# A kernel's head rearranged: the second load of V on SyncE, V's rows split over three engines, both W1 folds in front of the first MLP product

## The chip, the cores and the metric

The kernel runs on one core of one Trainium2 chip. A core has a matrix engine (TensorE, PE in the profile, with its weight loads as PEld), VectorE (DVE), ScalarE (ACT), GpSimd (POOL) and SyncE (SP). Each takes its instructions in order; semaphores connect them. DMAs are issued from the queues of SP, ACT and POOL. TensorE writes its products to PSUM, and DVE or ACT bring them from there to SBUF. The metric is the device time of the core in microseconds, as the median of several executions; smaller is better.

## The reference

The input x has 8 images of 3136 rows and 256 columns. What is computed is the real part of a two-dimensional Fourier transform, then a low-rank mixing over the rows, then an MLP over the columns with a residual:

```python
X = np.fft.fft(x, axis=1)
X = np.fft.fft(X, axis=2).real          # (8, 3136, 256)
xt = X.transpose(0, 2, 1)
h = xt @ U @ V                          # U (3136, 32), V (32, 3136)
u = X + h.transpose(0, 2, 1)
out = u + np.maximum(u @ w_ch1, 0.0) @ w_ch2   # 256 -> 1024 -> 256
```

## The kernel before

The 3136 rows are taken as 49 x 64 (`N1`, `N2`), and only 25 values of `k1` (`NK1`) are transformed, since the input is real; the other 24 follow by symmetry. The images go in four pairs. Every image passes these steps: a first transform over 49 rows, a turn of the layout into `g` (128 rows of 25 x 256), a transform over 64 rows that multiplies `g` with the table `T` and at the same time adds the low-rank part, and the MLP. Rows 0 to 63 of `T` are sine and cosine values; rows 64 to 127 are V, in two copies: as it is, in the columns 0 to 63 (the plus rows), and turned and with a sign on a part of the rows, in the columns 64 to 127 (the minus rows). Rows 64 to 127 of `g` hold `te`, the product of the image with U, repeated for all 25 `k1`: this repetition is called the spread. So the product of `g` and `T` gives u. It comes out in PSUM and is copied as bf16 to `q`.

The MLP works on chunks of 512 columns of `q`. `mlp1(chunk, t)` makes a quarter of the hidden layer, four products of 128x512 into a PSUM buffer `hps`, which ACT brings to `hT` with the ReLU (L385). `mlp2(chunk, t)` multiplies `hT` with `W2` and adds the residual from the tables `Bp` or `Bm` (L394, L397). The weights `W1p` (two halves of 512 columns, used by t = 0, 1 and by t = 2, 3) are not w_ch1 itself: the transform over the columns is folded into them by a product of the table `Q` with a half of w_ch1 (`w1_fold`, L668, four matmuls in fp32r) and a scaling by 0.5. `W2` is w_ch2 with its halves added and subtracted (`w2_fold`, L531).

The order is written out by hand (`tc.manual_schedule()`, L461): each engine takes its instructions as the Python code issues them. The code ahead of the loop (L463 to L722) is the head: it builds all tables, loads the weights and takes the first image as far as `q`. In the loop (L815) every step t of a chunk issues `mlp1`, the previous chunk's `mlp2` and then the functions that the list `at` holds for this step (L773 to L813): for the first pair, among others, the rest of the first image's transform (`s3b0`), the folds of W2 and the late tables.

What matters around the change, in the order of the code:

- V is loaded twice into `uv`, fp32 and 32 rows each, rows 64 to 95 (L495) and rows 96 to 127 (L627), both from POOL's queue. The second stands behind the one-element copy `gate` (L617), which waits for a table of DVE, and ahead of the load of W1's first half (L624).
- The table `T` gets its upper rows from PSUM by four DVE copies (L614), and its reversed half by one more (L660).
- The residual's angles are made on POOL, masked on DVE (`bp_mask`, L661) and taken through the sine on ACT (`bp_sin`, L688).
- A second one-element copy `gate` (L662) on POOL waits for a late row of `g0`.
- `w1_fold(0)` (L675) stands ahead of the products for `te` (`te_single`, L693).
- `v_rows` (L678) writes V's rows into `T`: `k1` 0 to 8 on ACT, 9 to 16 and 17 to 24 on POOL. Each call makes the plus rows by a cast, L681 or L684, and the minus rows by a multiply with the sign column `vs`, L682 or by `tg`, L514. The read goes through `Vk`, which steps by 49 fp32 elements.
- The first eight `k1` are multiplied in two passes, first with the 64 table rows, then with all 128 rows and `te` (L698 to L701), and moved to `q` in two parts, blk 0 by ACT and blk 1 by DVE (L702).
- `w1_late` (L706) runs behind the first `mlp1`: the second fold into two PSUM tiles of the transform's pool, its scaling by two DVE instructions, and the spread of `k1` 8 to 15 on DVE. POOL spreads `k1` 16 to 24 (L713) and then loads the next image (L716).
- `jio` and `Q` come from two SBUF pools. `kpool` and `pool` (for `tmp`) both end with the head, and the buffers of the loop (`q` of the other pair, `hT`, `ob`) lie over them; a buffer's first writer waits for the last readers of what lay there.
- PSUM buffers come from three pools of two: `bank2` (shared with `hps`), `bank_d` (the transform) and `bank_o` (shared with `mlp2`).

Of the kernel before, what the change touches and what calls it, by code (L numbers as in the profile page):

```python
# [11 lines left out]
FP32R = mybir.dt.float32r  # L12
I32 = mybir.dt.int32
# [9 lines left out]
def kernel(  # L23
# [51 lines left out]
    def copy_dve(o, i):  # L75
        nc.vector.tensor_copy(o, i)  # L76
# [352 lines left out]
    def tmp(shape, name, dt=FP32):  # L429
        return pool.tile(shape, dt, name=name, tag=name)  # L430
# [35 lines left out]
    next(loads)  # L466
    pio = tmp([P, 1], "pio", I32)
    nc.gpsimd.iota(pio[:], pattern=[[0, 1]], base=0, channel_multiplier=1)
    jio = kpool.tile([P, D], I32, name="jio", tag="jio")
    nc.gpsimd.iota(jio[:], pattern=[[1, D]], base=0, channel_multiplier=0)  # L470
    uv = kpool.tile([P, S], FP32, name="uv", tag="uv")
    uf = kpool.tile([P, 1024], FP32, name="uf", tag="uf")[:, 0:NK1 * R].rearrange("p (k r) -> p k r", r=R)
# [7 lines left out]
    def bank2(name):  # L480
        return psh.tile([P, 2, 512], FP32, tag="h", name=name)

    def bank_d(name):
        return psd.tile([P, 2, D], FP32, tag="ps", name=name)
# [108 lines left out]
        ts(an2[:, i], jf[0:PR, 0:32], pv[:, 6:7], pv[:, 7 + i:8 + i])  # L593
    mask_bits(an2[:], 16)
    mask_bits(jq[:], 16)
    Q = tmp([P, 3, P], "Q", FP32R)

    usv = us[:].rearrange("p k (r s) -> p k s r", s=2)
    upss = [bank2("uups") for i in range(2)]
# [12 lines left out]
    for i in range(4):  # L612
        k0, k1 = 8 * i, min(8 * i + 8, NK1)
        copy_dve(T[0:64, k0:k1, 0:64], tpss[i][0:64, 0:k1 - k0])  # L614

    gate = tmp([64, 4], "gate")
    nc.gpsimd.tensor_copy(gate[0:1, 0:1], an2[0:1, 0, 0:1])  # L617
# [6 lines left out]
        nc.gpsimd.dma_start(out=w, in_=moe_w_ch1.rearrange("(h p) j -> p h j", p=P)[:, :, c * 512:(c + 1) * 512])  # L624
        return w

    nc.gpsimd.dma_start(out=uv[96:128], in_=moe_V)  # L627
    w1_f = [load_w1(0)]

    g0 = gpool.tile([P, NK1, D], BF16, tag="g0", name="g")  # L630
# [27 lines left out]
    outs[1](copy_act)  # L658
    quarter_rows(g0, zts[1], 16, [copy_dve] * 6 + [copy_act] * 2)
    nc.vector.tensor_copy(T[0:64, :, 64:128], T[0:64, :, 63::-1])  # L660
    bp_mask()  # L661
    nc.gpsimd.tensor_copy(gate[32:33, 2:3], g0[32:33, 0, 80:81])  # L662

    teps = bank2("teps")
    for i in range(5):
# [9 lines left out]
    w1_fold(0, [w1ps[:, 0], w1ps[:, 1]])  # L675
    Vk = uv.rearrange("p (k2 k1) -> p k1 k2", k1=N1)

    def v_rows(lo, hi, act=False):  # L678
        l = max(lo, 1)
        if act:  # L680
            nc.scalar.copy(T[64:128, lo:hi, 0:64], Vk[64:128, lo:hi, :])  # L681
            nc.scalar.activation(T[64:128, l:hi, 64:128], Vk[64:128, N1 - l:N1 - hi:-1, :], AF.Copy, scale=vs[64:128])  # L682
        else:
            nc.gpsimd.tensor_copy(T[64:128, lo:hi, 0:64], Vk[64:128, lo:hi, :])  # L684
            tg(T[64:128, l:hi, 64:128], Vk[64:128, N1 - l:N1 - hi:-1, :], vs[64:128], None)

    v_rows(0, 9, True)
    bp_sin()  # L688
    nc.scalar.mul(W1p[0][:], w1ps[:], 0.5)
    v_rows(9, 17)  # L690
    v_rows(17, NK1)

    te_single(first, 0, lambda g, te: None, teps)  # L693
    s3b0 = list(s3_steps(first, 0, copy_alt))
    lines, move_part = s3b0.pop(0)
    groups = [(g, blk) for g in range(2) for blk in range(2)]
    pss = [bank("ps") for bank in [bank_d, bank_d, bank_o, bank_o]]
    for ps, (g, blk) in zip(pss, groups):  # L698
        lines(ps, g, blk, 64)
    for ps, (g, blk) in zip(pss, groups):  # L700
        lines(ps, g, blk, P, tes[0])  # L701
    for part in range(2):  # L702
        for ps, (g, blk) in zip(pss, groups):
            move_part(ps, g, blk, copy_dve if blk else copy_act, part)

    def w1_late():  # L706
        w1ps = [bank_d("w1ps").rearrange("p a d -> p (a d)") for blk in range(2)]
        w1_fold(1, w1ps)
        for blk in range(2):
            ts(W1p[1][:, blk], w1ps[blk], 0.5, None)  # L710
        spread([(nc.vector, 8, 16)])(g0, tes[0])

    spread([(nc.gpsimd, 16, NK1)])(g0, tes[0])  # L713
    idx0 = cpool.tile([PR, 8 * NP], I32, name="idx0")
    nc.gpsimd.iota(idx0[:], pattern=[[PR * 16, NP], [-1, 8]], base=48 * 16 + 15, channel_multiplier=-16)
# [57 lines left out]
    def plan(p):  # L773

        at = [[] for _ in range(NS)]

        def place(steps, lo, hi):
            steps = list(steps)
            for i, s in enumerate(steps):
                at[lo + i * (hi - lo) // len(steps)].append(s)  # L780

        def place_next(nx, a, gap, s3lo):

            s1 = list(s1_steps(nx, copy_act))
# [77 lines left out]
```

## Time and profile before

| what | value |
|---|---|
| median of 6 runs | 460.75 us (459.8 to 466.6) |
| profiled execution | 463.08 us, span 461.3 us |
| granted TensorE clock, mean | 0.991 |
| PE busy | 432.2 us, 94% of the span |
| ACT, DVE, POOL busy | 297.3, 225.0, 142.2 us |
| HBM read, written | 34.62 and 32.19 MB, 145 GB/s |
| share of the DMA engines, 13.5 to 15 us and 15 to 16.5 us | 0.4 and under 0.1 |
| PE busy between 30.8 and 36.9 us | 4.05 us of 6.10 |

The span runs from the first to the last instruction of the profiled execution; its own time has 1.8 us around it. Busy shares are means over stages with different limits: the head, up to about 37 us, has all engines at work in turn, while later PE is nearly always busy. The timeline gives for every line its start and its length in us, then engine, source line, operation, the tiles written and read with their shapes, the count, and in brackets the idle time of the engine ahead of it with what ended it. The waits give engine, line and releaser, then the total in us, how often, and the longest.

The operations of the head that the change moves, as the profile gives them:

| instruction | where | us |
|---|---|---|
| V cast, 64x576 | ACT | 1.22 |
| V times sign, 64x512 | ACT | 1.19 |
| V cast, 64x512 | POOL | 1.08 |
| V times sign, 64x512 | POOL | 2.06 |
| spread 64x1024 / 64x1152 | DVE / POOL | 1.03 / 1.49 |
| W1p scaling 128x512 from PSUM | DVE | 0.685 |
| W1p scaling 128x1024 from PSUM | ACT | 1.00 |
| second load of V, 392 KB | POOL queue | 0.60 to issue, 4.1 to land |
| one half of W1, 512 KB | POOL queue | 0.76 to issue, 4.6 to 4.9 to land |

### The profile page before, as it was taken

To read this page: it belongs to the slowest core of one execution; us is meant where nothing else is said; L and a number is where in the kernel's file an instruction comes from. 1 tells how busy PE (TensorE), PEld (TensorE's weight loads), DVE (VectorE), ACT (ScalarE), POOL (GpSimd) and SP (SyncE) were. 2 spreads that over 40 slices of the span, in tenths; PEclk is the share of its full clock that TensorE was granted. 3 is DMA by queue.
4 is the path that set the end of the run, shared out by engine and by line. 5 is a ranking of instruction groups with operands and counts; after the bars stand their busy time and mean duration, and the time that the engine had idled before them with its cause. 6 is when DMAs were issued, how large, how long until landed. Compare 5 with 4: busy or idle time off the path is not lost.

```text
span 461.3 us, 10592 instructions
## 1 busy us (share of the span) xinstructions
PE 432.2 (94%) x4217; PEld 309.7 (67%) x4217; DVE 225.0 (49%) x540; ACT 297.3 (64%) x426; POOL 142.2 (31%) x159
## 2 busy tenths in 40 slices
PE   3889996999989989999999989999999999999994
PEld 1756664777767767767767767776867777677663
DVE  7674567664336476455354386436254345111212
ACT  5776884777555666777465657777566655666662
POOL 7484535751330363452330354452220000000000
PEclk9799999999999999999999999999999999999999
DMA  8649754785492547673862447674752222222313
GB/s 149 149 135 164 212 153 110 207 207 171 134 251 56 155 121 233 182 209 116 196 173 70 111 155 215 167 234 128 182 128 66 68 62 65 70 73 72 91 47 92
DMA packets 59714, 64.35 MB, mean 139 GB/s; under 512 B 12902, under 2 KB 52624, under 8 KB 59504
## 3 DMA queue, kind: packets, MB, share of 16 engines
q1 hardware_dynamic: 49904, 42.28, 35.6%
q0 software_dynamic: 7280, 14.70, 13.8%
q10 hardware_dynamic: 2480, 6.69, 3.9%
q8 instruction: 33, 0.54, 0.5%
q14 instruction: 17, 0.14, 0.1%
HBM read 34.62 MB, written 32.19 MB: 145 GB/s over the span
## 4 chain that ended last, share of the span: by engine, by line
PE 65%; DMA 9%; DVE 7%; ACT 4%; SPq 4%; issue 2%; DVEq 0%; ACTq 0%
PE hps L383 27%; PE ops L394 27%; DMA out_dram<-ob 4%; PE ps L322 4%; SPq L409 4%; PE ops L397 3%; DMA xa<-in_x_dram 3%; ACT hT L385 2%; PE ps L184 2%; DVE g L76 2%; DMA g<-zturn 1%; DVE ob L405 1%; DVE q L76 1%; DVE yb L134 1%; DVE ob L404 1%
## 5 line engine op out<-in xcount | busy, mean ns | idle before, releaser
L385 ACT ACTIVATE hT<-hps 128x1024 bf16<-128x1024 f32 (+1 forms) x208 | 202.4, 976 | 122.5 <-PE hps L383 118.0
L394 PE MATMUL ops<-W,hT 128*128 128x256 bf16 x1568 | 224.7, 273 | 0.6 <-DVE W L532 0.3
L394 PEld LDWEIGHTS <-hT 128*128 128x128 bf16 x1568 | 145.1, 98 | 35.0 <-DVE ob L405 0.8
L404 DVE TENSOR_TENSOR ob<-ops,om 128x256 f32<-128x256 f32 (+1 forms) x102 | 42.2, 413 | 192.2 <-ACT om L403 183.8
L383 PE MATMUL hps<-q,W1p 128*128 128x512 bf16 (+1 forms) x448 | 105.0, 356 | 0.9 <-DVE q L76 0.6
L383 PE MATMUL hps<-q,W1m 128*128 128x512 bf16 x384 | 98.1, 379 | 0.5 <-ACT hT L385 0.5
L143 POOL TENSOR_TENSOR y<-xa,xb 98x1020 f32<-98x1020 f32 (+1 forms) x24 | 55.1, 2297 | 126.2 <-DMA xa<-in_x_dram 108.5
L76 DVE CAST q<-ps 128x512 bf16<-128x512 f32 (+3 forms) x121 | 64.4, 555 | 28.9 <-PE ps L322 27.6
L383 PEld LDWEIGHTS <-W1p 128*128 128x128 bf16 x448 | 40.3, 98 | 26.6 <-issue 1.7
L383 PEld LDWEIGHTS <-W1m 128*128 128x128 bf16 x384 | 35.3, 98 | 26.5 <-issue 1.4
L397 PEld LDWEIGHTS <-q 128*128 128x128 bf16 x392 | 38.4, 98 | 21.3 <-issue 0.6
L403 ACT COPY om<-ops 128x256 f32<-128x256 f32 (+1 forms) x102 | 37.1, 364 | 8.1 <-PE ops L394 7.7
L405 DVE TENSOR_TENSOR ob<-ops,om 128x256 f32<-128x256 f32 (+1 forms) x102 | 41.1, 403 | 0.0
L322 PE MATMUL ps<-T,g 128*128 128x128 bf16 (+3 forms) x400 | 36.9, 218 | 3.0 <-DMA g<-zturn 1.2
L73 ACT CAST z<-ps 128x512 bf16<-128x512 f32 x48 | 28.2, 588 | 17.4 <-PE ps L184 17.1
L397 PE MATMUL ops<-Bp,q 128*128 128x128 f16 x200 | 38.4, 219 | 0.0
L306 POOL COPY g<-te 64x1024 int32<-64x1024 int32 (+1 forms) x22 | 23.1, 1092 | 46.5 <-DVE te L270 42.9
L397 PE MATMUL ops<-Bm,q 128*128 128x128 f16 x192 | 36.9, 219 | 0.0
L322 PEld LDWEIGHTS <-g 128*128 128x128 bf16 (+1 forms) x400 | 29.2, 98 | 8.3 <-issue 1.9
L99 POOL DMA_INDIRECT xb<-in_x_dram,idx x24 | 26.0, 1082 | 5.4 <-issue 4.1
L184 PE MATMUL ps<-yb,F 98*128 98x258 bf16 (+1 forms) x108 | 18.9, 265 | 6.5 <-DVE q L76 4.8
L134 DVE TENSOR_TENSOR yb<-y 98x508 bf16<-98x508 f32 (+1 forms) x24 | 23.4, 975 | 1.0 <-POOL y L143 1.0
(137 smaller groups left out, 219.8 us busy)
## 6 DMA issues: line engine op xcount, KB each, us to landing
out_dram<-ob SPq DMA_DIRECT2D x389, 64.0 KB
xa<-in_x_dram SPq DMA_DIRECT2D x24, 392.0 KB
g<-zturn SPq DMA_DIRECT2D x6, 800.0 KB
zturn<-z ACTq DMA_DIRECT2D x9, 512.0 KB
X<-in_x_dram POOLq DMA_DIRECT2D x4, 384.0 KB, 7.7
X<-in_x_dram POOLq DMA_DIRECT2D x2, 744.0 KB, 8.0
zturn<-z ACTq DMA_DIRECT2D x3, 448.0 KB
w_f<-in_moe_w_ch_dram POOLq DMA_DIRECT2D x2, 512.0 KB, 4.7
```

The costliest lines, as they stand in the source:

```text
L73: nc.scalar.copy(o, i)
L76: nc.vector.tensor_copy(o, i)
L143: nc.gpsimd.tensor_tensor(ck.y[:, 0:n, 1:256], ck.xa[:, 0:n, 1:256], rb[:, :, 255:0:-1], op=AL.add)
L184: nc.tensor.matmul(o[..., cs], F[:, 2 * t + i].rearrange("p b k c -> p (b k c)"), y[..., cs], start=first, stop=True, skip_group_check=True)
L322: nc.tensor.matmul(o, lt, r, start=st, stop=True, skip_group_check=True)
L383: nc.tensor.matmul(ps[:, i, 0:n], (W1p if ch.sg > 0 else W1m)[jp // 2][:, blk, j], q[:, blk, c0:c0 + n], start=(blk == 0), stop=(blk == 1))
L385: nc.scalar.activation(ch.h[:, 2 * jp:2 * jp + 2, 0:n], ps[:, :, 0:n], AF.Relu)
L394: nc.tensor.matmul(ps, ch.h[:, j, t * P:(t + 1) * P], W2[:, j, :], start=(j == 0 and (t % 2 == 0 or last)), stop=(j == JT - 1), skip_group ...
L397: nc.tensor.matmul(ps[:, j], q[:, j, tk], (Bp if ch.sg > 0 else Bm)[:, j], start=False, stop=False, skip_group_check=True)
L403: nc.scalar.copy(om[:, 0:n], ch.po[:, 0:n, 1])
L404: nc.vector.tensor_tensor(ob[:, 0:n, 0:P], ch.po[:, 0:n, 0], om[:, 0:n], op=AL.add)
L405: nc.vector.tensor_tensor(ob[:, 0:n, P:D], ch.po[:, 0:n, 0], om[:, 0:n], op=AL.subtract)
```

## The change

The second load of V is issued from SP, behind the third of four DVE copies into `T`; a one-element memset on DVE in the destination makes it wait for that place. V's plus rows 9 to 16 and 17 to 24 and minus rows 9 to 16 are written by DVE; POOL keeps the minus rows 17 to 24 and takes the spread of `k1` 8 to 15, ahead of them. The mask and the sine of the residual table stand later, behind the products for `te`. Both W1 folds are made ahead of the first MLP product; the second goes into a buffer of `bank2`, and one DVE instruction scales it, between the two parts of the moves to `q`. The second `gate` is gone. The folds of W2 come one step earlier in the list. `jio` and `Q` change pools. No arithmetic is added or left out, and the number of matmuls is the same.

```diff
-    jio = kpool.tile([P, D], I32, name="jio", tag="jio")
+    jio = tmp([P, D], "jio", I32)
...
-    Q = tmp([P, 3, P], "Q", FP32R)
+    Q = kpool.tile([P, 3, P], FP32R, name="Q", tag="Q")
...
         copy_dve(T[0:64, k0:k1, 0:64], tpss[i][0:64, 0:k1 - k0])
+        if i == 2:
+            nc.vector.memset(uv[96:97, 0:1], 0.0)
+            nc.sync.dma_start(out=uv[96:128], in_=moe_V)
...
-    nc.gpsimd.dma_start(out=uv[96:128], in_=moe_V)
     w1_f = [load_w1(0)]
...
-    bp_mask()
-    nc.gpsimd.tensor_copy(gate[32:33, 2:3], g0[32:33, 0, 80:81])
...
-    def v_rows(lo, hi, act=False):
+    def v_plus(lo, hi, copy):
+        copy(T[64:128, lo:hi, 0:64], Vk[64:128, lo:hi, :])
+
+    def v_minus(lo, hi, scale):
         l = max(lo, 1)
...
-    v_rows(0, 9, True)
-    bp_sin()
+        scale(T[64:128, l:hi, 64:128], Vk[64:128, N1 - l:N1 - hi:-1, :], vs[64:128])
+
+    v_plus(0, 9, copy_act)
+    v_minus(0, 9, lambda o, i, s: nc.scalar.activation(o, i, AF.Copy, scale=s))
     nc.scalar.mul(W1p[0][:], w1ps[:], 0.5)
-    v_rows(9, 17)
-    v_rows(17, NK1)
+    v_plus(9, 17, copy_dve)
+    v_minus(9, 17, lambda o, i, s: ts(o, i, s, None))
 
     te_single(first, 0, lambda g, te: None, teps)
...
+    bp_mask()
+    bp_sin()
+    v_plus(17, NK1, copy_dve)
...
         lines(ps, g, blk, P, tes[0])
+    w1ps = bank2("w1ps")
+    w1_fold(1, [w1ps[:, 0], w1ps[:, 1]])
     for part in range(2):
         for ps, (g, blk) in zip(pss, groups):
             move_part(ps, g, blk, copy_dve if blk else copy_act, part)
-
-    def w1_late():
-        w1ps = [bank_d("w1ps").rearrange("p a d -> p (a d)") for blk in range(2)]
-        w1_fold(1, w1ps)
-        for blk in range(2):
-            ts(W1p[1][:, blk], w1ps[blk], 0.5, None)
-        spread([(nc.vector, 8, 16)])(g0, tes[0])
-
+        if part == 0:
+            ts(W1p[1][:], w1ps[:], 0.5, None)
+    spread([(nc.gpsimd, 8, 16)])(g0, tes[0])
+    v_minus(17, NK1, lambda o, i, s: tg(o, i, s, None))
     spread([(nc.gpsimd, 16, NK1)])(g0, tes[0])
...
-            at[0].append(w1_late)
...
-            at[1].append(lambda: w2_fold(0))
-            at[3].append(lambda: w2_fold(1))
+            at[0].append(lambda: w2_fold(0))
+            at[2].append(lambda: w2_fold(1))
```

More of the change, by code (lines that the diff above doesn't have):

```diff
@@ L676 @@
     Vk = uv.rearrange("p (k2 k1) -> p k1 k2", k1=N1)
-    def v_rows(lo, hi, act=False):
+    def v_plus(lo, hi, copy):
+        copy(T[64:128, lo:hi, 0:64], Vk[64:128, lo:hi, :])
+    def v_minus(lo, hi, scale):
         l = max(lo, 1)
[L680 to L685, printed above, removed]
-    v_rows(0, 9, True)
-    bp_sin()
+        scale(T[64:128, l:hi, 64:128], Vk[64:128, N1 - l:N1 - hi:-1, :], vs[64:128])
+    v_plus(0, 9, copy_act)
+    v_minus(0, 9, lambda o, i, s: nc.scalar.activation(o, i, AF.Copy, scale=s))
     nc.scalar.mul(W1p[0][:], w1ps[:], 0.5)
-    v_rows(9, 17)
-    v_rows(17, NK1)
+    v_plus(9, 17, copy_dve)
+    v_minus(9, 17, lambda o, i, s: ts(o, i, s, None))
     te_single(first, 0, lambda g, te: None, teps)
```

## The prediction

> **What bounds the kernel now.** I read the page first (busy shares by slice and the chain that ended last), then the chain and the waits of the head, then the timeline of the head engine by engine, since everything the change touches lies before 37 us.
>
> ```profile
> PE   3889996999989989999999989999999999999994
> PE 65%; DMA 9%; DVE 7%; ACT 4%; SPq 4%; issue 2%; DVEq 0%; ACTq 0%
> ```
>
> TensorE (PE) is busy nearly everywhere and carries 65% of the chain. Followed back inside the first 55 us, the chain is unbroken PE work from 36.8 us, the first second-layer product (L394), to about 49 us. So what the head is worth is the moment at which that product starts. The waits between 20 and 40 us, and the timeline lines behind them:
>
> ```profile
> ACT hT L385 <- issue: 1.6, 1, 1.6
> PE ps L322 <- DVE g L306: 1.1, 1, 1.1
> PE hps L383 <- DVE q L76: 0.6, 1, 0.6
> PE hps L383 <- ACT q L73: 0.3, 1, 0.3
> PE ops L394 <- DVE W L532: 0.3, 1, 0.3
> ```
>
> ```profile
> 24.08 0.58 DVE L660 COPY T<-T 64x1600 bf16<-64x1600 bf16 x1
> 24.12 0.56 POOL L662 CAST gate<-g 1x1 f32<-1x1 bf16 x1 [1.89 <-DVE g L76]
> 25.74 0.29 DVE L269 CAST te<-teps 32x129 bf16<-32x129 f32 x1 [0.88 <-PE teps L298]
> 26.57 1.01 PE L322 MATMUL ps<-T,te 128*128 128x64 bf16 x16
> 27.18 1.47 DVE L76 CAST q<-ps 128x256 bf16<-128x256 f32 x4 [0.85 <-PE ps L322]
> 27.93 1.02 PE L383 MATMUL hps<-q,W1p 128*128 128x512 bf16 x4 [0.34 <-ACT q L73]
> 28.60 1.28 PE L671 MATMUL w1ps<-w_f,Q 128*128 128x512 f32 x4
> 29.46 1.29 DVE L443 TENSOR_SCALAR W1p<-w1ps 128x512 bf16<-128x512 f32 x2 [0.81 <-PE w1ps L671]
> 29.97 1.94 ACT L385 ACTIVATE hT<-hps 128x1024 bf16<-128x1024 f32 x2 [1.59 <-issue]
> 30.77 1.03 DVE L306 COPY g<-te 64x1024 int32<-64x1024 int32 x1
> 31.84 2.05 DVE L532 TENSOR_TENSOR W<-w_f 128x1024 bf16<-128x1024 f32 x1
> 31.86 0.40 PE L322 MATMUL ps<-T,g 128*128 128x128 bf16 x4 [1.10 <-DVE g L306]
> 34.96 0.69 DVE L76 CAST q<-ps 128x512 bf16<-128x512 f32 x1 [0.47 <-PE ps L322]
> 35.56 1.21 DVE L532 TENSOR_TENSOR W<-w_f 128x1024 bf16<-128x1024 f32 x1
> 36.83 0.27 PE L394 MATMUL ops<-W,hT 128*128 128x256 bf16 x1 [0.32 <-DVE W L532]
> ```
>
> PE is idle 0.4 us between 27.6 and 30.8, and 2.05 us between 30.8 and 36.9 (busy 2.83 of 3.20 and 4.05 of 6.10). Those 2.4 us, 0.5% of the run, are all that the edit can win here. The biggest piece is a chain on VectorE (DVE): late W1 fold (ends 29.88), its scaling (29.46 to 30.75), the spread of te into g rows 8 to 15 (30.77 to 31.80), and only then the next transform matmul (31.86). The first ReLU sits 1.6 us: its product ended at 28.95, but it started at 29.97, 0.09 after the fold's end; in the built program it waits for that fold, because hT lies over Q.
>
> **The change part by part.**
>
> *V load from SyncE (SP).* It issues behind the third T copy on DVE (3 x 0.67 from 13.34, so 15.1, plus 0.06 for the memset), about 15.2. The queues carry nothing between 15 and 16.5. The same load on POOL took 4.1 us to land; another V load under full queues 10.1 (median of the two 7.1). I take 4.1, since the queues stand empty: landed at 19.3, first reader at 23.59. At 10.1 it lands at 25.3 and costs 1.7. Behind it on SP stand the 12.5 KB row (18.32) and the W2 load (22.26); an issue is under 0.85 us, so both keep their time. On POOL's queue W1's first half goes 0.6 earlier; its fold at 22.85 follows PE work without a wait, so nothing is won there. The memset lies in DVE's 2.27 us pause before 17.62. Cost nothing; cover 4.3 us on the load, 2.1 on the memset.
>
> *V rows 9 to 16 on DVE, in front of te.* Two 64x512 reads of fp32 with a step of 49 elements. DVE does no such read now. Below stands 0.42 us (two elements a cycle, as the 98x384 table multiply at 0.375 suggests: 0.15 fixed plus 0.27); in the middle 0.68, the 64x512 cast from PSUM; above 1.08 and 2.06, the same two operations on POOL. ScalarE (ACT) takes 1.22 for 576 and 1.19 for 512 of this read, against 0.78 for a 64x576 cast from PSUM. The Trainium skill, "SBUF — State Buffer", section "Specifications (TRN2)", says that full bandwidth needs at least two hits on a 16-byte line; here each element is in another line. An estimate from that page with one port is two cycles an element, 1.2 us; the ACT rows fit it. "VectorE: DVE Perf Modes", "Mode 2×_2P", says that a one-source copy within SBUF reads through both ports, which brings 1.2 back to 0.7. I take 0.68. Then te starts at 24.66 + 1.36 = 26.02 instead of 25.74, ends 26.6, and the te matmuls start at 26.65 instead of 26.57. At 1.22 each te ends at 27.67 and the matmuls lose 1.1.
>
> *V rows 17 to 24.* Plus rows on DVE behind the mask (26.6 + 0.2), 0.68, so q copies from 27.5; before 27.18. Here a rule speaks against the change: the same SBUF page, "Who interferes with whom", gives DVE in two-port mode and GpSimd (POOL) one exclusive lock, and POOL's spread is released by the same te. The trace agrees: the one-element gate took 0.56 instead of 0.29 and ended with DVE's T copy (24.68, 24.66); the first W2 fold took 2.05 instead of 1.21 beside POOL's 31.32 to 32.81. If POOL gets in first (1.04 for 64x1024), q starts at 28.5. PE has the fold until 28.8 by then, so the sum loses only about 0.25.
>
> *Spread of rows 8 to 15 on POOL, minus rows behind it.* 26.8 to 27.9, minus rows 2.06 to 29.9, spread of rows 16 to 24 1.19 to 31.1. That takes the 1.03 off DVE's chain. POOL drops the second gate, two plus rows and one minus row (0.56 + 2.17 + 2.06) and is free 1.7 earlier (31.1 for 32.81), so the next image's loads go out earlier; their reader is at 50.0, so no gain.
>
> *Mask and Bp sine.* Sine behind W1p on ACT: q copies at 27.35 instead of 27.24. Bp is read first at 36.94.
>
> *Fold in front of the product.* 27.5 to 28.8 (pitch 1.26 as at 22.85). W1's second half was issued at 21.22 and lands by 26.1. The product t=0 follows at 28.8 instead of 27.93. A new wait: the product t=1 takes the PSUM buffer that the fold used, so it waits for the scaling: 28.85 plus 1.2 (0.15 + 1.07 for 1024 in one piece), 30.1; before 29.72. Then nothing is missing: transform at 31.0 (31.86 before), t=2 at 31.25 (32.10), t=3 at 32.55 (33.41). The first ReLU starts at 29.8, no longer held by the fold.
>
> *W2 folds.* First 30.8; POOL reads until 31.1, so done at 32.3; q 32.5 to 33.15; second fold to 34.35; q for chunk 1 to 35.03; its product's last three matmuls 35.07 to 35.72. The first second-layer product starts at about 35.7 instead of 36.83.
>
> **Sum:** 1.1 earlier; 0.85 if the lock goes to POOL. I take 1.0. The profiled execution took 463.08 (span 461.3, 1.8 around it) and would become 462.1. It is 2.3 above the median of 460.75; the same 1.0 off the median gives 459.75, which I round to 459.7. What follows the head is released by instruction order, so it moves with it.
>
> **The rivals.** *The strided read is dear, or the gain is given back.* At 1.22 each on DVE, the te matmuls start at 27.7, t=1 at 31.25, the second-layer product at 36.65: 0.2 won, 460.5. The ACT rows speak for it, two ports against. The same figure follows if later waits for x loads (7.5 us of chain at 190) absorb the earlier start; against that, those loads follow the stores, which move too.
>
> *Slower: DVE reads V no faster than POOL.* Place: V rows ahead of te. With POOL's 1.08 and 2.06, te ends at 28.4, fold 30.5, t=1 31.9, second-layer product 37.55: 0.7 lost, 461.4. With 2.06 for all three it is 2.4, 463.1. It decides from about 1.3 us per 512 elements, since te moves by two such reads. Against it: DVE beats POOL on every comparable row (te spread 1.03, POOL 1.49).
>
> *The change doesn't do what it says.* If the buffer wait on t=1 were longer than reckoned, or the lock fell on the mask too, PE idles at 28.8 to 30.1 instead of 30.8; zero, 460.7. *All idle goes:* 2.4, 458.4; against it, the W2 folds and the buffer wait remain.
>
> **How the numbers follow.** Main case 0.55 (459.7, own range 459.2 to 460.2 before scatter); dear read or gain absorbed 0.27 (460.5); slower 0.13 (461.4, to 463.1); more than the sum 0.05 (458.4). The six runs scatter above 459.8, with the middle two 0.9 apart, so the ends widen by about 0.6: 458.3 to 461.9. A change of 1% is 4.6 us, about what a measurement of this kernel can tell from none. The whole idle time of the place is half of that, and the dearest reckoning loses 2.4; only something outside the head could pass it. Faster 0.03, within 0.92, slower 0.05.
>
> **What would show it.** Right: first second-layer product near 35.7; no wait of the transform for g; first ReLU within 0.1 of its product; V copies on DVE near 0.7; t=1 held by the scaling. Wrong: te matmuls after 27, a V copy over 1.2, a stretched copy beside POOL's spread, ACT waiting for V at 23.6, or a head that ends earlier with an unchanged end.

## The result, and the profile after

| | before | after |
|---|---|---|
| median of all executions | 461.34 us (71) | 460.44 us (34) |
| ratio, 95% interval | 1 | 0.9974 [0.9959, 0.9989] |
| profiled execution, its span | 463.08, 461.3 us | 462.87, 461.1 us |
| granted TensorE clock of it, mean | 0.991 | 0.986 |
| first product for `te` (L298) | 24.11 us | 26.33 us |
| first second-layer product (L394) | 36.83 us | 37.75 us |
| from the one to the other | 12.72 us | 11.42 us |

The ratio is worth 1.2 us, between 0.5 and 1.9: within 1%, where the prediction took 1.0. It leaves out the executions that lie more than 1.5% above the fastest of their kernel, while the medians are of all. The profiled pair alone would mislead. Its spans differ by 0.2 us and the head ends later than before, though the part of the head that the change rearranges has become 1.3 us shorter.

The page of the kernel after, the busy tenths of PE and the chain's shares by engine:

```profile
PE   3699996999989999999999989999999999999994
PE 73%; DVE 9%; DMA 9%; ACT 3%; issue 2%; SPq 2%; POOL 1%; DVEq 0%; ACTq 0%; POOLq 0%
```

Nothing has changed in kind: TensorE bounds the kernel. The first three digits are the head, 11.5 us each. Before, they were 3, 8 and 8: the third slice, with the rearranged part, has become fuller, and the second, ahead of it, emptier. The waits of the kernel after between 20 and 40 us:

```profile
PE tps L226 <- issue: 1.7, 1, 1.7
ACT hT L385 <- issue: 1.3, 1, 1.3
...
PE hps L383 <- DVE q L76: 0.5, 1, 0.5
...
PE hps L383 <- DVE W1p L443: 0.3, 1, 0.3
...
PE ps L322 <- ACT q L73: 0.3, 1, 0.3
```

Against the list of before, the transform's wait of 1.1 us for the spread on DVE is gone, and the second-layer product no longer waits for `W2`. In their place stand 0.3 us for the scaling of `W1p`, 0.3 us for a copy to `q`, and, at the top, a wait that the prediction had not thought of: 1.7 us of "issue" in the first transform (L226), ahead of everything the change moves. The other "issue", of the first ReLU, is no loss: the timeline shows it starting as its product ends. The timeline of the kernel after:

```profile
15.37 2.91 PE L226 MATMUL tps<-Fs,X 98*32 98x50 f16 x125 [2.20 <-DMA X<-in_x_dram]
...
18.39 0.66 PE L226 MATMUL tps<-Fs,X 98*32 98x100 f16 x7
20.71 2.73 PE L226 MATMUL tps<-Fs,X 98*32 98x100 f16 x115 [1.67 <-issue]
...
26.33 1.59 PE L298 MATMUL teps<-g,us 64*32 64x129 bf16 x50
26.88 0.61 DVE L76 CAST T<-uv 64x512 bf16<-64x512 f32 x1
...
27.41 0.67 DVE L443 TENSOR_SCALAR T<-uv,vs 64x512 bf16<-64x512 f32 x1
...
28.64 1.16 POOL L306 COPY g<-te 64x1024 int32<-64x1024 int32 x1 [5.79 <-DVE te L270]
...
28.79 1.01 PE L322 MATMUL ps<-T,te 128*128 128x64 bf16 x16
28.93 1.34 DVE L76 CAST T<-uv 64x512 bf16<-64x512 f32 x1
...
29.61 1.18 PE L671 MATMUL w1ps<-w_f,Q 128*128 128x512 f32 x4
...
30.30 0.76 DVE L76 CAST q<-ps 128x256 bf16<-128x256 f32 x2
...
30.64 1.28 PE L383 MATMUL hps<-q,W1p 128*128 128x512 bf16 x4
30.97 1.21 DVE L443 TENSOR_SCALAR W1p<-w1ps 128x1024 bf16<-128x1024 f32 x1
...
32.00 1.02 ACT L385 ACTIVATE hT<-hps 128x1024 bf16<-128x1024 f32 x1 [1.31 <-issue]
...
32.24 1.02 PE L383 MATMUL hps<-q,W1p 128*128 128x512 bf16 x4 [0.32 <-DVE W1p L443]
...
32.81 1.67 DVE L532 TENSOR_TENSOR W<-w_f 128x1024 bf16<-128x1024 f32 x1
...
33.10 0.39 PE L322 MATMUL ps<-T,g 128*128 128x128 bf16 x4
...
37.10 0.81 PE L383 MATMUL hps<-q,W1p 128*128 128x512 bf16 x3 [0.47 <-DVE q L76]
...
37.75 0.27 PE L394 MATMUL ops<-W,hT 128*128 128x256 bf16 x1
```

Read it in two halves. Up to 26.33 stands code that the change touches only by the load of V; there the kernel after is 2.22 us later in this execution. From 26.33 on stands the rearranged part: two cheap reads of V on DVE (0.61 and 0.67), a third that takes twice as long beside the spread on POOL (1.34), the fold in front of the product, one wait for its scaling (0.32), and a transform that no longer waits for `g`; its third group waits 0.28 for a copy to `q`.

The same rounds in the timeline of the kernel before:

```profile
14.95 2.58 PE L226 MATMUL tps<-Fs,X 98*32 98x50 f16 x126 [1.11 <-ACT us L73]
...
17.60 0.65 PE L226 MATMUL tps<-Fs,X 98*32 98x100 f16 x7
18.53 2.73 PE L226 MATMUL tps<-Fs,X 98*32 98x100 f16 x115 [0.28 <-issue]
```

The 2.22 us have three parts, all in the first transform's two rounds. Against before, the first round starts 0.42 later (15.37 for 14.95), takes 0.38 longer (its last matmuls end at 19.05 for 18.25), and the second round is held for 1.67 instead of 0.28. That is 2.19, and nothing is added behind it.

So two questions were left for experiments: which parts of the change shorten the stretch from L298 to L394, and whether the load on SP lengthens what stands ahead of it.

### The profile page after: what moved, and what is told of

It reads as the page before. It is cut to its first block, busy times and chain, and to the rows that moved or that the text cites. A ratio compares the mean times of both kernels' runs of the same rounds, so it can differ in the third digit from the quotient of the medians.

```text
span 461.1 us, 10588 instructions
## 1 busy us (share of the span) xinstructions
PE 432.0 (94%) x4217; PEld 309.9 (67%) x4217; DVE 225.1 (49%) x542; ACT 297.3 (64%) x426; POOL 137.2 (30%) x155
## 4 chain that ended last, share of the span: by engine, by line
PE 73%; DVE 9%; DMA 9%; ACT 3%; issue 2%; SPq 2%; POOL 1%; DVEq 0%; ACTq 0%; POOLq 0%
PE hps L383 31%; PE ops L394 30%; DMA out_dram<-ob 4%; PE ops L397 4%; PE ps L322 3%; PE ps L184 2%; ACT hT L385 2%; DMA X<-in_x_dram 2%; SPq L409 2%; DVE q L76 2%; DMA g<-zturn 2%; PE teps L284 1%; DVE g L76 1%; PE tps L226 1%; DVE ob L404 1%
## 5 line engine op out<-in xcount | busy, mean ns | idle before, releaser
L394 PE MATMUL ops<-W,hT 128*128 128x256 bf16 x1568 | 224.7, 273 | 0.3 <-DVE ob L405 0.3
L394 PEld LDWEIGHTS <-hT 128*128 128x128 bf16 x1568 | 145.1, 98 | 35.0 <-DVE ob L405 0.8
L306 POOL COPY g<-te 64x1024 int32<-64x1024 int32 (+1 forms) x23 | 23.9, 1081 | 54.8 <-DVE te L270 51.3
L99 POOL DMA_INDIRECT xb<-in_x_dram,idx x24 | 24.9, 1039 | 5.4 <-issue 4.2
```

The source lines that it names most:

```text
L394: nc.tensor.matmul(ps, ch.h[:, j, t * P:(t + 1) * P], W2[:, j, :], start=(j == 0 and (t % 2 == 0 or last)), stop=(j == JT - 1), skip_group ...
```

## Experiments

The timed intervals are 2 to 3 parts in a thousand to each side, about 1 us. That is as large as the whole effect, so they decide no part of it, and after and after_again, which are one kernel, lie 0.003 apart. The stretch from the first L298 to the first L394 in each trace is finer: it holds only head work, and the two traces of the kernel after agree within 0.07 us. The granted clock is whole between L298 and L394 in all of these traces but that of late_and_act. Both are given.

| kernel | ratio to before, 95% | span of its trace | L298 | L298 to L394 |
|---|---|---|---|---|
| before | | 461.3 | 24.11 | 12.72 |
| before_again | 1.0015 [0.9985, 1.0046] | 459.8 | 24.27 | 12.13 |
| load_only | 0.9998 [0.9976, 1.0020] | 464.1 | 25.84 | 12.74 |
| vrows_only | 0.9961 [0.9933, 0.9990] | 458.7 | 23.91 | 12.38 |
| folds_only | 0.9962 [0.9938, 0.9985] | 460.0 | 24.52 | 11.81 |
| after | 0.9974 [0.9959, 0.9989] | 461.1 | 26.33 | 11.42 |
| after_again | 0.9944 [0.9919, 0.9969] | 462.7 | 25.57 | 11.49 |
| load_pool | 0.9969 [0.9940, 0.9998] | 458.5 | 24.06 | 11.99 |
| load_late | 0.9970 [0.9947, 0.9992] | 460.9 | 24.49 | 11.47 |
| load_double | 0.9978 [0.9952, 1.0003] | 461.6 | 26.12 | 11.42 |
| vplus_late | 0.9961 [0.9940, 0.9983] | 461.5 | 25.90 | 11.55 |
| scale_act | 0.9935 [0.9911, 0.9960] | 458.0 | 24.01 | 11.22 |
| late_and_act | 0.9953 [0.9926, 0.9979] | 456.7 | 23.27 | 13.12 |

### Both kernels once more

before_again and after_again are the two kernels unchanged, to see how much a trace scatters.

> The kernel before once more, for a second trace of it. Theory A (the te products of the first image, L298, started late in the profile after, 26.3 for 24.1 us, by chance of that one execution): here too their start scatters, somewhere between 24 and 26 us. Theory B (the V load in the pause of the queues holds back the transfer of TensorE's instructions, 18.0 for 15.6 us, and so the transform that starts at 18.5): here the instruction transfer comes near 15.6 again, and L298 starts within 0.5 us of 24.1. Both: from L298 to the first second-layer product (L394) 12.7 us, within 0.3; ratio 1.00.

> The changed kernel once more. Theory A: L298 starts somewhere between 24 and 26 us, not tied to the V load. Theory B: an instruction transfer near 18 us again, a TensorE stall of about 1.7 us behind it, L298 near 26.3. Both: from L298 to the first L394 11.4 us, within 0.3; ratio 0.997 to the kernel before.

The stretch of the kernel after came out the same (11.49). That of the kernel before was 0.6 shorter than in its first trace: the spread on DVE took 0.73 instead of 1.03 and the first fold of `W2` 1.23 instead of 2.05, as the timeline of before_again shows:

```profile
30.90 0.73 DVE L306 COPY g<-te 64x1024 int32<-64x1024 int32 x1
31.66 1.23 DVE L532 TENSOR_TENSOR W<-w_f 128x1024 bf16<-128x1024 f32 x1
```

Both are the operations that ran beside POOL in the first trace; here POOL was done earlier. So a part of what the change seems to win in the first pair is given or taken by chance in the kernel before. The three traces with the old order from L298 on (before, before_again, load_only) average 12.53, and the change wins 1.07 of that, or between 0.6 and 1.3 against the single traces. load_late and load_double below keep the new order from L298 on and have 11.47 and 11.42, so the gain of the stretch is not chance of one trace.

The lateness ahead of L298 came again in after_again (25.57, with a first round at 15.57 and a second at 20.61), which made the load on SP the suspect.

### The load of V back to POOL, and the load alone

load_pool is the kernel after with the load where it was:

```diff
         copy_dve(T[0:64, k0:k1, 0:64], tpss[i][0:64, 0:k1 - k0])
-        if i == 2:
-            nc.vector.memset(uv[96:97, 0:1], 0.0)
-            nc.sync.dma_start(out=uv[96:128], in_=moe_V)
...
+    nc.gpsimd.dma_start(out=uv[96:128], in_=moe_V)
     w1_f = [load_w1(0)]
```

> The changed kernel with the second V load back on GpSimd's queue in front of W1's first half; all else as changed. Theory A: the load costs and wins nothing, so the time stays within 0.3 us of the changed kernel, and no wait for V appears. Theory B: the instruction transfer comes near 15.6 us, the stall of 1.7 us goes, L298 starts near 24.1, and the time falls by 1.5 to 2 us against the changed kernel (ratio 0.993 to before).

load_only is the kernel before with nothing but this load moved (the same edit the other way round).

> The kernel before with only the second V load moved to SyncE, behind the third T copy. Theory A: ratio 1.000 within 0.001, from L298 to the first L394 12.7 us as before. Theory B: the instruction transfer comes near 18 us, TensorE stalls, L298 starts near 26.3, and the time rises by 1.5 to 2 us (ratio 1.004).

In the traces the suspicion holds: load_pool reaches L298 at 24.06, load_only at 25.84. The timeline of load_only, the two rounds of the first transform on PE:

```profile
15.61 2.52 PE L226 MATMUL tps<-Fs,X 98*32 98x50 f16 x127 [2.51 <-POOL pq L453]
...
20.27 2.73 PE L226 MATMUL tps<-Fs,X 98*32 98x100 f16 x115 [1.41 <-issue]
```

It is the picture of the kernel after without any of its other edits: a first round at about 15.5 and a stall of 1.4 us that no semaphore explains. But the times don't follow: load_only stands at 0.9998 and load_pool at 0.9969, beside 0.9974 and 0.9944 for the kernel with the load on SP. If 1.7 us were lost in every execution, load_only would be at 1.004, outside its interval. And load_pool, with the load on POOL, has a stall of 1.44 us at its second round all the same, and 0.39 us of "issue" within the L298 products, which is why its stretch is 11.99.

### The two halves of the rearrangement

folds_only is the kernel before with the second fold in front of the first product; the V rows, the load, the mask and the spread of `k1` 8 to 15 stay as they were:

```diff
+    w1ps = bank2("w1ps")
+    w1_fold(1, [w1ps[:, 0], w1ps[:, 1]])
     for part in range(2):
         for ps, (g, blk) in zip(pss, groups):
             move_part(ps, g, blk, copy_dve if blk else copy_act, part)
-    def w1_late():
...
+        if part == 0:
+            ts(W1p[1][:], w1ps[:], 0.5, None)
+    spread([(nc.vector, 8, 16)])(g0, tes[0])
```

> The kernel before with only the folds changed: the second fold in front of the first product, scaled in one piece, Q and jio in the other pools; V rows, their load and the spread on VectorE as before. Our theory (the gain needs the spread to leave VectorE): scaling 28.9 to 30.1, q copies to 30.75, spread to 31.8, so the transform with g still starts about 7.7 us after L298 and nothing is won: from L298 to the first L394 12.1 to 12.7 us as in the two traces before, ratio 1.000. Rival (the first ReLU's wait for the late fold was the loss): it goes, and the whole gain of about 1 us comes with it, 11.4 to 11.6 us, ratio 0.997.

vrows_only is the kernel after with the second fold back behind the first product, in two pieces, and the folds of `W2` one step later, as before; the load on SP, the V rows on three engines and the spread on POOL stay:

```diff
-    w1ps = bank2("w1ps")
-    w1_fold(1, [w1ps[:, 0], w1ps[:, 1]])
...
+            at[0].append(w1_late)
...
-            at[0].append(lambda: w2_fold(0))
-            at[2].append(lambda: w2_fold(1))
+            at[1].append(lambda: w2_fold(0))
+            at[3].append(lambda: w2_fold(1))
```

> The changed kernel with the second fold late again, behind the first product and scaled in two pieces; V rows, spread on GpSimd and the load as changed. Our theory: the transform no longer waits for a spread on VectorE, but the fold's PSUM buffers hold it until the scaling has read them; from L298 to the first L394 about 12.0 us, half of the gain, ratio 0.998. Rival (the ReLU's wait): Q lies in the pool that the ReLU doesn't wait for here, so all of the gain is there without the early fold, 11.5 us, ratio 0.997.

folds_only took 11.81, between the two expectations; vrows_only took 12.38, more than either. The timeline of folds_only shows where the spread on DVE still holds the transform:

```profile
29.02 1.23 DVE L443 TENSOR_SCALAR W1p<-w1ps 128x1024 bf16<-128x1024 f32 x1 [0.56 <-PE w1ps L671]
...
30.30 1.02 PE L383 MATMUL hps<-q,W1p 128*128 128x512 bf16 x4 [0.44 <-DVE W1p L443]
...
30.87 0.69 DVE L306 COPY g<-te 64x1024 int32<-64x1024 int32 x1
...
31.62 0.40 PE L322 MATMUL ps<-T,g 128*128 128x128 bf16 x4 [0.29 <-DVE g L306]
```

With the fold moved ahead, its scaling starts 0.85 us earlier relative to L298 (4.50 behind it for 5.35), and the spread behind it runs unblocked in 0.69. The wait for `g` is 0.29 instead of 1.10 (0.80 in before_again). The larger part of the gain comes with the fold alone: 0.7 of 1.07 against the mean of the old order. It is one trace, and against the single traces of the old order it is 0.3 to 0.9.

The timeline of vrows_only, with the spread on POOL but the folds late:

```profile
30.02 1.29 DVE L443 TENSOR_SCALAR W1p<-w1ps 128x512 bf16<-128x512 f32 x2 [0.76 <-PE w1ps L671]
...
34.42 0.69 DVE L76 CAST q<-ps 128x512 bf16<-128x512 f32 x1 [1.05 <-PE ps L322]
35.03 1.21 DVE L532 TENSOR_TENSOR W<-w_f 128x1024 bf16<-128x1024 f32 x1
...
36.29 0.27 PE L394 MATMUL ops<-W,hT 128*128 128x256 bf16 x1 [0.32 <-DVE W L532]
```

The transform no longer waits for the spread, but what is won there is lost before L394: the second fold of `W2` stands behind the last copy to `q`, DVE is idle for 1.05 us ahead of that copy, and L394 waits for the fold as it did before. Against the mean of the old order, taking the spread off DVE is worth 0.15 us as long as the folds of `W2` keep their place; with a scatter of 0.6 between traces of that order, this is not distinct from nothing. With the fold (0.7) the two alone make 0.85; the whole change makes 1.07. It also issues the folds of `W2` one step earlier, which neither run does and no run tests alone: in both L394 still waits 0.32 for `W2`, and in the kernel after it does not. That this is the remaining 0.2 is likely, but not shown.

### Scaling on ScalarE

The longer of the two new waits of the kernel after is that of the second product for the scaling on DVE, which starts late behind the stretched V copy. scale_act gives the scaling to ACT, behind the moves:

```diff
-        if part == 0:
-            ts(W1p[1][:], w1ps[:], 0.5, None)
+    nc.scalar.mul(W1p[1][:], w1ps[:], 0.5)
```

> The changed kernel with the scaling of W1's second half on ScalarE instead of VectorE. Theory (the second product waits for this scaling, because its PSUM buffer is the fold's): it starts 0.3 us earlier, since ScalarE takes 1.0 us for 1.2 and stands idle there, and from L298 to the first L394 11.1 us for 11.4. Rival (the last copies to q set the end): the second product is earlier, but the first L394 is not, 11.4 us. The time moves by less than its interval in both.

The stretch was 11.22, and the timeline of scale_act shows why it is not less:

```profile
28.32 2.29 PE L383 MATMUL hps<-q,W1p 128*128 128x512 bf16 x7
28.51 1.02 ACT L708 ACTIVATE W1p<-w1ps 128x1024 bf16<-128x1024 f32 x1 [0.25 <-PE w1ps L671]
...
30.05 2.15 DVE L532 TENSOR_TENSOR W<-w_f 128x1024 bf16<-128x1024 f32 x1 [0.67 <-DMA w_f<-in_moe_w_ch_dram]
...
34.59 0.81 PE L383 MATMUL hps<-q,W1p 128*128 128x512 bf16 x3 [0.60 <-DVE q L76]
```

Seven matmuls of the first two products run in one piece, so the wait of 0.32 is gone. DVE comes to the first fold of `W2` so early that it waits 0.67 us for the weights' DMA, and then shares its time with POOL's spread (2.15 us for 1.22 alone). The product of chunk 1 waits 0.60 for the last copy to `q` instead of 0.47. Its ratio, 0.9935, is the lowest of all, but its interval overlaps that of the kernel after: a win over it isn't shown.

### The V copy behind the moves

vplus_late moves the V copy that met the spread on POOL behind the moves to `q`:

```diff
-    v_plus(17, NK1, copy_dve)
...
             ts(W1p[1][:], w1ps[:], 0.5, None)
+    v_plus(17, NK1, copy_dve)
```

> The changed kernel with V's plus rows 17 to 24 on VectorE behind the copies to q instead of ahead of them. Theory (the lock between VectorE and GpSimd stretched this copy to 1.34 us and held the first product): the second half of the first product no longer waits for q, and the first product takes 1.0 us for 1.28; but the scaling of W1 keeps its place, so from L298 to the first L394 11.3 us for 11.4, and the copy meets GpSimd again at its new place. Rival (the lock costs the end its full 0.7 us): 10.8 us. Ratio as the changed kernel in both.

The timeline of vplus_late:

```profile
30.21 1.04 PE L383 MATMUL hps<-q,W1p 128*128 128x512 bf16 x4
...
32.24 0.93 DVE L76 CAST T<-uv 64x512 bf16<-64x512 f32 x1
...
33.20 1.23 DVE L532 TENSOR_TENSOR W<-w_f 128x1024 bf16<-128x1024 f32 x1
...
36.81 0.81 PE L383 MATMUL hps<-q,W1p 128*128 128x512 bf16 x3 [0.73 <-DVE q L76]
```

The first product takes 1.04 instead of 1.28, as expected. But the copy costs 0.93 at its new place, the first fold of `W2` moves from 6.48 to 7.30 us behind L298, and the product of chunk 1 waits 0.73 instead of 0.47. (The second product, too, comes only 0.13 earlier behind L298, 5.78 for 5.91: its wait for the scaling is 0.43.) The stretch is 11.55: the quarter microsecond is handed on, not won.

### The load of V later, and doubled

Two more kernels ask what the load on SP does to the first transform. load_late issues it behind the last copies of the first round (at 19.66 us in its trace), so that its data can't meet the stall:

```diff
-        if i == 2:
-            nc.vector.memset(uv[96:97, 0:1], 0.0)
-            nc.sync.dma_start(out=uv[96:128], in_=moe_V)
...
+    nc.vector.memset(uv[96:97, 0:1], 0.0)
+    nc.sync.dma_start(out=uv[96:128], in_=moe_V)
```

> The changed kernel with the SyncE load of V later, behind VectorE's copy of the first transform at about 18.2 us and so behind W1's first half. Theory B (V in the pause holds back TensorE's instructions in the profiled execution): the instruction transfer comes near 15.6 us, the stall in front of the second transform round shrinks, and L298 starts at 24 to 24.7 us for 25.6 to 26.3. Theory A (chance): L298 anywhere between 24 and 26.3, the instruction transfer near 18 as likely as near 16. V lands at about 23 and is waited for by 0.5 us at most. Ratio 0.995 to 0.997 in both.

load_double issues it two copies earlier and adds a second load of 352 KB of V into a tile that nobody reads:

```diff
-        if i == 2:
+        if i == 0:
+            spare = pool.tile([P, 2816], FP32, name="spare", tag="spare")
             nc.vector.memset(uv[96:97, 0:1], 0.0)
+            nc.vector.memset(spare[96:97, 0:1], 0.0)
             nc.sync.dma_start(out=uv[96:128], in_=moe_V)
+            nc.sync.dma_start(out=spare[96:128], in_=moe_V[:, 0:2816])
```

> The changed kernel with the V load on SyncE behind the first T copy instead of the third, and behind it a second load of 352 KB of V that nothing reads, so that the queues carry data from about 14.9 to 18 us. Theory C (an instruction transfer of TensorE falls due about 0.7 us after the first transform round starts, and is held back when V's data are on the queues then; in the changed kernel they are there from 16.2, so it depends on when the round starts): the transfer comes at 17.5 to 18.5 us, the second transform round about 2.7 us after it, L298 at 25.5 to 26.5 us. Rival (V's load has nothing to do with it): transfer at 15.2 to 16.0, L298 at 24 to 24.7. If the delay also holds outside the profiled execution, the ratio is 0.998 to 1.000, otherwise 0.995 to 0.997.

The traces list the DMA queues. One of them, called "instruction" (q8), carries a transfer of 0.02 MB between 15 and 18.3 us, read here in windows of 0.15 us, of which the start is given (the expectations name times read in windows of 0.4 us). The second round of the first transform starts 2.3 to 3.0 us behind it wherever the two rounds stand apart:

| kernel | V load | first round | transfer | second round |
|---|---|---|---|---|
| before | POOL | 14.95 | 15.85 | 18.53 |
| before_again | POOL | 14.36 | 15.25 | 17.56 |
| load_pool | POOL | 14.94 | 16.00 | 18.93 |
| folds_only | POOL | 15.01 | 16.00 | 18.93 |
| late_and_act | SP, late | 14.62 | 15.55 | 18.18 |
| load_late | SP, late | 15.01 | 15.85 | no pause |
| scale_act | SP | 14.57 | 15.40 | 18.39 |
| vrows_only | SP | 14.74 | 15.70 | no pause |
| after | SP | 15.37 | 18.10 | 20.71 |
| after_again | SP | 15.57 | 17.95 | 20.61 |
| load_only | SP | 15.61 | 17.80 | 20.27 |
| vplus_late | SP | 15.44 | 17.95 | 20.55 |
| load_double | SP, twice | 14.90 | 16.90 | 19.51 |

The transfer comes 0.8 to 1.1 us behind the start of the first round in the first eight rows, and 2.0 to 2.7 behind it in the last five. In these five, V's data are on the queues at the time at which the transfer would come by the measure of the first eight; in scale_act and vrows_only, with the same load, the first round starts early enough that the transfer is through before V's data come at 16.1 us.

load_late reaches L298 at 24.49, and ACT's first read of V there (23.80) comes without a wait, so the load issued 4.5 us later was still covered. The DMA list of the kernel after for 14 to 20 us, the queues with packets, MB and share of 16 engines:

```profile
DMA  1414002000000099330999600309435997799994
...
q1 hardware_dynamic: 48, 0.40, 26.1%
q8 instruction: 1, 0.02, 1.3%
```

The digits are 0.15 us each. The queue q1 carries V, and its data fills the engines at 16.1 to 16.4 and at 16.9 to 17.3, while in the kernel before the same list is empty from 15 to 17.7 us but for one digit, the small transfer itself. The small transfer comes behind V's data in the kernel after, and ahead of any load in the kernel before. load_double is the direct test: its first round starts at 14.90, almost as in before, and the transfer comes at 16.90 instead of 15.85. The timeline of load_double:

```profile
14.90 2.15 PE L226 MATMUL tps<-Fs,X 98*32 98x50 f16 x128 [1.06 <-ACT us L73]
...
19.51 2.73 PE L226 MATMUL tps<-Fs,X 98*32 98x100 f16 x115 [2.06 <-issue]
```

The stall is 2.06, the longest but for that of vplus_late (2.55). Its length alone says little, since a first round at whole clock ends sooner and leaves a longer pause: load_pool, also at whole clock there, has 1.44. But the transfer is about 1 us later than with the load on POOL, and the second round 0.6 us later than in load_pool and 1.0 later than in before. So V's data can delay both even when the first round is on time; it is one trace, and the other four late ones agree with it. The delay was less than expected (the transfer at 16.9 for 17.5 to 18.5), so the delay doesn't grow simply with the bytes on the queues.

What the runs don't explain is why four of six executions with the load on SP at the place of the change start the first round at 15.37 or later, and none of the others does. That round waits for the first image (X), whose load ends at 15.1 in the chain of the kernel after, ahead even of the issue of V (15.19) and a microsecond ahead of V's first data. And load_double, with V issued at 14.16, starts that round at 14.90. In the timed runs nothing of the delay shows: load_late stands at 0.9970, load_double at 0.9978, both beside the kernel after, but a microsecond is 0.002 and no more than these intervals. Whether executions without the profiler have the stall is open.

### Load late and scaling on ScalarE together

late_and_act joins the edits of load_late and scale_act, as a candidate for a better version.

> The changed kernel with the SyncE load of V behind VectorE's copy of the first transform and the scaling of W1's second half on ScalarE. Theory: the two add: L298 at 24 to 24.7 us and from there to the first L394 11.1 to 11.3 us, ratio to the kernel before 0.993 to 0.996. Rival (the scaling's gain was one trace's luck): 11.4 us or more, ratio 0.996 to 0.998.

Its median, 459.46 us, is the lowest of its round, with that of vplus_late (459.66) next; its ratio 0.9953 is no better than that of scale_act, and its stretch was 13.12, the longest of all. The timeline of late_and_act:

```profile
23.98 1.21 ACT L73 CAST T<-uv 64x576 bf16<-64x576 f32 x1 [1.40 <-DMA uv<-in_moe_V_dram]
...
26.35 1.71 PE L322 MATMUL ps<-T,te 128*128 128x128 bf16 x15 [0.35 <-ACT T L685]
...
27.81 1.96 PE L670 MATMUL w1ps<-w_f,Q 128*128 128x512 f32 x4
```

ACT waits 1.40 us for V. Issued at 18.27, the load lands only at about 23.9, and this execution comes to L298 early (23.27), so its cover is gone. The rest is the clock. Stretches of late_and_act: window, its length, then busy time and instructions of PE, PEld, DVE, ACT and POOL, the granted clock, the DMA share and GB/s:

```profile
25.00:26.00 1.00, 0.99 (x16) 0.76 (x14) 0.95 (x4) 1.00 (x2) 0.27 (x1) 1.00 1.01 343
26.00:27.00 1.00, 0.65 (x9) 0.65 (x8) 0.98 (x1) 0.98 (x2) 0.89 (x2) 0.56 1.08 386
27.00:28.00 1.00, 1.00 (x11) 1.00 (x10) 0.79 (x2) 0.97 (x3) 1.00 (x1) 0.50 0.47 160
```

From 26.1 us TensorE is granted half its clock, and the 16 matmuls with `te` and the fold, whose lengths sum to 2.2 us in the kernel after, take 3.9. This execution still had the shortest span of all, 456.7 us: the head and the rest of one execution say little about each other.

## Why the prediction was right, point by point

**The load of V.** Its data was on the queues from 16.1 to 17.4 us and its first reader came at 25.77, so the load itself cost nothing, as said. The price put on it, nothing, left out what else travels on these queues. That the empty pause also held an instruction transfer was not in the working; in the profiled executions it is late by 2.25 us (18.10 for 15.85, of which 0.42 is the later round), and in the timed ones no loss can be seen.

**V rows 9 to 16 on DVE.** 0.61 and 0.67, for 0.68 each taken between 0.42 and 2.06. The rival of a dear read is refuted: DVE reads fp32 with a step of 49 elements as fast as it casts from PSUM, where ACT pays 1.22 for 0.78. That the second port does this, as the working had it, isn't shown; the time is. The `te` matmuls come 2.46 us behind L298, as predicted (26.65 less 24.11 is 2.54).

**V rows 17 to 24 and the lock.** The prediction left open who gets in first: POOL did, by 0.29 us, in after, vrows_only, scale_act and late_and_act alike. The copy took 1.34 instead of 0.61, and the copies to `q` began at 30.30, for 30.7 with the lock lost (all positions here are the predicted ones plus 2.22, for the later L298). The Trainium skill, "SBUF — State Buffer", section "Who interferes with whom", was the weight on that side, and the trace agrees with it in order and size: the copy, 0.61 alone, ends 0.47 behind POOL's spread. The price reckoned for it was 0.25 of the sum. At the first product it is that, 1.04 in vplus_late for 1.28; at L394 it can't be seen: L394 came at 37.75, where the working, moved by 2.22, has 37.9 without the loss and 38.2 with it, and vplus_late wins nothing there, because its copy costs 0.93 at the other place.

**Fold, buffer wait, transform.** The second product started at 32.24 (predicted 32.3, held by the scaling of 1.21, as predicted), the transform at 33.10 (33.2), the third product at 33.32 (33.5), the fourth at 35.07 (34.8; it waited 0.28 for ACT). The first ReLU started 0.08 us behind its product, no longer held by the fold over whose tile `hT` lies.

**The folds of W2.** The first began at 32.81 (33.0) and took 1.67 beside POOL (1.5 reckoned); L394 came at 37.75 for 37.9, with a wait of 0.47 for `q` in the product ahead of it, where before there were 0.57 for `q` and then 0.32 for `W2`.

**The sum.** 0.85 to 1.1 us were predicted for the stretch. It shrank by 1.30 in the profiled pair and by 1.07 against the mean of the three traces of the old order; the timed ratio says 1.2, between 0.5 and 1.9, and after_again, the same kernel, 2.6. The clock is not the reason: the mean granted clock of the timed executions is 0.9916 in after_again and 0.9912 in the kernel before beside it. By single traces the fold's place makes 0.7 of it and the V rows with the spread 0.15 or nothing; the remaining 0.2 came with the whole change, the earlier folds of `W2` among it, and was not taken apart. That the timed gain is this stretch and nothing else isn't shown: the intervals are too wide to add parts up.

**The number and the range.** That the time fell into the range is weak support. The range, 458.3 to 461.9, holds an unchanged 460.75 as well, and the median measured, 460.44, is nearest to the 460.5 of the rival. It is so because the six executions before had a median of 460.75 and the 71 of the comparison one of 461.34; the ratio is what counts. What speaks for the working are the positions in the traces.

**The step that failed** is the silent one that all before L298 stays in place. In the profiled execution it came 2.22 later, by the first round, its stall and the clock. Three of the prediction's own signs of being wrong came with it and with the lock: `te` matmuls after 27 (28.79, by this lateness), a V copy over 1.2 (1.34), and this copy stretched beside POOL's spread. None of them undid the gain in the stretch. "What follows the head moves with it" holds in the order of instructions but can't be seen in single traces: from L394 to the end the thirteen executions took between 420.3 (late_and_act) and 425.6 us (after_again), though that code is the same in all. A gain of 1 us can be read in the head and in many timed runs, and not from two spans.

**The rival that gives back the gain** predicted 0.2 us. The interval, from 0.5 on, speaks against it, by a small margin; its second form, that later waits absorb the gain, the traces can't test, since what follows L394 scatters by 5 us. The slower rival needed a read of more than 1.3 us, and the reads took half of that.

## What to carry to other kernels

When an engine's queue holds a later stage's input behind a slow chain, first find what stands in front of it in its own queue: here moving one fold ahead of the product won about 0.7 us by starting DVE's chain earlier, while taking work off that engine won 0.15 at most as long as the next wait stayed. Price a moved copy with the engine that will be running beside it, since a V copy of one shape took 0.61, 0.93 or 1.34 us at three moments. And measure a gain of a microsecond in a short stretch between two fixed instructions, over several traces; the span of one execution scatters by more.

## What the runs showed of the hardware that was not expected

**Half clock in steps of 3.41 us.** In the head the granted TensorE clock is either whole or half. Read in half-microsecond windows, it was half from 15.93 to 22.75 us in before (6.82), from 14.87 to 25.11 in after (10.24), from 15.66 to 19.07 in after_again (3.41), from 14.45 to 17.86 in scale_act (3.41), from 21.30 to 24.71 in vplus_late (3.41) and from 19.30 to 26.13 in load_double (6.83); in before_again and load_pool it stays whole up to 33 us. The second round of the first transform takes 2.73 us at half clock and 1.96 at whole. The Trainium skill, "TensorE: Matmul & The Clock Gate", Part 1, tells of a free-running window of 3413 ns, and the steps are its multiples. Its table of the two clock states asks for an idle window ahead of the half clock, and no such pause is in these traces: the longest idle time of PE ahead of a drop is 2.55 us (vplus_late), in before it is 1.11 us, and in late_and_act PE was busy 2.72 of the 3.41 us ahead of the drop. What sets off a drop stays open. The number of steps varies from execution to execution of one kernel (two in before, none in before_again; three in after, one in after_again), and the mean clock goes with the time. Of the 34 executions of the kernel after, the 14 with a mean clock under 0.9895 have a median of 461.26 us, the 9 from 0.9935 on 459.49.

**A load can put off a transfer of the queue "instruction", and a TensorE round with it.** A transfer of 0.02 MB that no line of the program asks for stands 2.3 to 3.0 us ahead of a TensorE round that no semaphore in the trace holds, and in load_double comes about 1 us later than in before at nearly the same start of the round. That it is TensorE's own code is inferred from this order, not read in the trace; what is measured is that it comes 0.8 to 1.1 us behind the start of the first round in eight traces, and 2.0 to 2.7 in the five in which 0.4 MB of V are under way at its time.

**A blocked DVE instruction ends almost its whole length behind POOL.** The V copy of 0.61 us ended 0.47 behind POOL's spread in the kernel after and 0.48 in vplus_late; the first fold of `W2`, 1.22 alone, ended 1.07 behind it in the kernel after and 1.08 in scale_act. All but 0.13 to 0.15 us of each length came behind POOL's end, so such a meeting is priced as one behind the other.

**Cost of one read by engine.** The fp32 read with a step of 49 elements took 0.61 to 0.68 us for 64x512 on DVE where nothing held it, 1.19 on ACT and 1.08 (copy) or 2.06 (multiply) on POOL.
